# Two steps, one or none of w2's maxima per product, PSUM of h emptied first, and the second filter unit behind a product

## The chip, the cores and the metric

The kernel runs on one core of one Trainium2 chip. What counts is the device time of one execution in microseconds (us), as the median of three runs. A profile of one more execution gives every instruction its place in time; all times below are counted from its first instruction.

## The reference

Two branches read one layer-normed input, and their product is added to the input. One is a filter in two-dimensional frequency space, the other a feed-forward layer with SiLU.

```python
x = A_x                                  # 1 x 2048 x 1024
xn = _layernorm(x, axis=-1)
s = irfft2(rfft2(xn) * (w_r + 1j * w_i)) # the filter, 2048 x 513 complex weights
h = _silu(xn @ B_w1)                     # w1: 1024 x 3584
g = _silu(h @ B_w2)                      # w2: 3584 x 1024
return x + s * g
```

## The kernel before

All matrix work is done in fp16 pairs, a high and a low half of each number, with three matmuls for one product of pairs. TensorE (PE) carries nearly the whole time; VectorE (DVE), ScalarE (ACT) and GpSimd (POOL) do the transforms' butterflies, the splits into halves and the scales; SyncE (SP) issues nearly all DMAs, in order, and waits at each until its data are there.

**Products.** The first layer is 112 products `mm1(c, f)`: a block c of 512 rows times a block f of 128 columns of w1, 24 matmuls into one bank of PSUM (`pa`). From the 25th on, products come in fours: two blocks f for two blocks c, which make one set (q, g) of h. Four PSUM buffers under the tag `ff` take turns, shared with the small matmuls of the column sums (`s`, L290). ACT empties a bank with the SiLU into `h` (L506, `evac`). After the fourth product of a set, `hidden` makes sums and differences of h on DVE (`hr`, L534, L535, L539), and `split` writes the halves of two groups: `hosum` (three arrays) and `hoone` (four). The high half is made on ACT (L281, `high`), the low one on DVE (L284, `low`), and both are stored to `hd` (L528). hosum and hoone have one buffer each.

**Slots.** The order of all engines is written out by the program. Behind each product `after` runs one slot: `settle` (the next stage of each set of h that is under way, then the emptying of the product before), `tick` (deferred DMAs), and `work`: a step of w1's preparation, then a step of the queue `xq`, then up to three steps of the queue `bg`, as long as a sum of estimated DVE costs is not ahead of the sum of PE costs by more than `LEAD`, or until a step returns `PAUSE`. Slots are counted by `count`; product n, counted from 0, has count n - 4.

In `settle` the stages of older sets stand first, and the emptying last:

```python
now, stages[:] = stages[:], []
if fresh_ev[0] is not None:
    now.append(fresh_ev[0])
```

**The queue xq** holds two generators, one after the other. `wmax_gen` takes 25 steps over the filter's weights: a load of 456 KB (`wm`) and a DVE reduction (L997), and a reduction over partitions on POOL. `w2max_gen` takes 31 steps over w2: a load of 128 rows (`w2m`, L403, 512 KB), three steps later the sums or differences of its halves on DVE (`wd`, L407, three buffers), which are stored for later use (`ws`, L408), and a sum of absolute values on ACT (`junk`, L414). Then POOL reduces over partitions. No load of the filter starts before this queue is done.

**The queue bg** holds, in order, the layer norms, the forward transforms `fd_gen(0)` to `fd_gen(3)`, the filter `f_gen` and the inverse transforms. A forward transform ends with four faces (`Rt`, `Ro`), each stored to `rd` (L929, `keep`) and added there once more by an indirect DMA of POOL (L934, `fold`), and for the last two transforms with small stores of an axis (`ao`, L960). Their ends lie near products 47, 67 and 86 for the second, third and fourth.

The filter works in 16 units. It loads data (`vr`, L1032, from `rd`), a table (`kq`, L1025) and weights (`wq`, L1049); `high_v` and `low_v` split vr into the halves of `vq`, on ACT and DVE; `mat` (L1061, `fx`) is the first use on PE. The first products of a unit stand in PE's order behind product 94, so that PE waits there for the low half of vq.

Of the kernel before, what the change touches and what calls it, by code (L numbers as in the profile page):

```python
# [29 lines left out]
SUMMED = (4, 5)  # L30
TURNED = (2, 3)
EXTRA = (20, 21, 22, 24)
ENTRY = ("fbwb||ew", "bbbwwbb|bwbb|f", "fwwbbw|wbbb|wb", "|wew|wf", "w||w")


# [115 lines left out]
def spectral_ffn(ctx, tc, x, w_r, w_i, w1, w2, ca, kc, ci, tw, pm, out):  # L151
# [48 lines left out]
    def defer(n, fn):  # L200
        deferred.append([n, fn])
# [78 lines left out]
    def high(hi, raw, scale):  # L280
        nc.scalar.activation(hi, raw, AF.Copy, scale=scale)  # L281
# [206 lines left out]
    def mm1(c, f, between={}):  # L488
        ps = pf.tile([128, 512], F32, name=f"pa{c}_{f}", tag="ff")
        w, xt = w1t[f], xnT[c]  # L490
        terms = [(d, wh, xh) for wh, xh in ((0, 0), (0, 1), (1, 0)) for d in range(8)]
        if f > 3 or c and f:
            terms.sort(key=lambda k: k[0])
        for n, (d, wh, xh) in enumerate(terms):
            if n in between:
                between[n]()
            nc.tensor.matmul(ps, w[:, wh, d], xt[:, xh, d], start=(n == 0), stop=(n == 23))  # L497
        if c == 3:
            used1.add(f)
        q, g = f // 2, c // 2  # L500

        def evac():
            if (q, g) not in h32:
                h32[q, g] = H["p"].tile([128, 4, 512], F32, name=f"h32_{q}_{g}", tag="h32", bufs=2)
            hq = h32[q, g]
            nc.scalar.activation(hq[:, 2 * (c % 2) + f % 2], ps, AF.Silu, scale=s1[:, f:f + 1])  # L506
            if c % 2 and f % 2:
                return hidden(q, g)

        return evac  # L510

    def hidden(q, g):

        hq = h32.pop((q, g))
        hp = H["p"]
        sc = hs[:, q:q + 1]
        tt = nc.vector.tensor_tensor

        def split(names, src):
            n = len(names)  # L520
            o = hp.tile([128, n, 4, 2, 128], F16, name=f"ho{names[0]}_{q}_{g}", tag=f"ho{n}", bufs=1)
            ov = [o[:, :, :, k] for k in range(2)]
            sv = src.rearrange("f o (p s) -> f o p s", p=4)
            high(ov[0], sv, sc)

            def rest():
                low(ov[1], sv, sc, ov[0])
                defer(2, lambda: nc.sync.dma_start(  # L528
                    hds[SETS.index(names), g][:, :, q].rearrange("f p h s -> f p (h s)"), o.rearrange("f k p h s -> f (k p) (h s)")))

            return rest

        sums = hp.tile([128, 3, 512], F32, name=f"hr{q}_{g}", tag="hr", bufs=1)
        tt(sums[:, 0:2], hq[:, 0::2], hq[:, 1::2], op=OP.subtract)  # L534
        tt(sums[:, 2], hq[:, 0], hq[:, 3], op=OP.subtract)  # L535

        def second():
            rest_s = split(SETS[0], sums)
            tt(hq[:, 2:0:-1], hq[:, 2:4], hq[:, 0:2], op=OP.subtract)  # L539

            def third():
                rest_h = split(SETS[1], hq)
                rest_s()
                return rest_h

            return third

        return second
# [471 lines left out]
    def f_gen():  # L1020
        bp = B["p"]

        def load_k(q):
            t_ = bp.tile([128, 4, 2, 128], F16, name=f"kq{q}", tag="K", bufs=2)
            (nc.sync if q else nc.gpsimd).dma_start(t_, kf[q])  # L1025
            B["k"][q] = t_

        def load_v(u):
            q, j = u // 4, u % 4
            t_ = bp.tile([128, 4, 2, 128], F32, name=f"vr{u}", tag="vr", bufs=2)  # L1030
            for side in range(2):
                nc.sync.dma_start(t_[64 * side:64 * side + 64], rows4[side][j][:, :, q])  # L1032
            raw[u] = t_.rearrange("m c r k -> m c (r k)")
# [3 lines left out]
        def high_v(u):  # L1037
            B["v"][u] = v = bp.tile([128, 4, 2, 256], F16, name=f"vq{u}", tag="vq", bufs=2)
            high(v[:, :, 0], raw[u], 2.0**-22)
# [5 lines left out]
        def load_w(u):  # L1045
            q, j = u // 4, u % 4
            for i in range(2):
                t_ = bp.tile([128, 4, 128], F32, name=f"wq{u}_{i}", tag="wq", bufs=4)
                nc.sync.dma_start(t_, wv[i][q][:, :, 128 * j:128 * j + 128])  # L1049
                B["w"][u, i] = t_  # L1050
# [3 lines left out]
        def mat(u):  # L1054
            q = u // 4
            v, k = B["v"].pop(u), B["k"][q]
            ps = pt.tile([128, 4, 2, 128], F32, name=f"fx{u}", tag="ft")
            for c in range(4):
                o = ps[:, c].rearrange("m r k -> m (r k)")
                for n, (kh, vh) in enumerate(((0, 0), (0, 1), (1, 0))):  # L1060
                    nc.tensor.matmul(o, k[:, c, kh], v[:, c, vh], start=(n == 0), stop=(n == 2))  # L1061
            psx[u] = ps

        load_k(0)
        load_v(0)
        load_w(0)
        yield PAUSE
        load_v(1)
        load_w(1)
        load_k(1)  # L1070
        yield PAUSE
        yield PAUSE
# [14 lines left out]
        def low_z(u):  # L1087
# [3 lines left out]
            if j == 3:  # L1091
                zv = zq.rearrange("m h (c n) i -> m h c (n i)", c=4)
                for c in range(4):
                    defer(1, lambda c=c: nc.sync.dma_start(zd[c][:, q], zv[:, :, c]))

        high_v(0)
        high_v(1)
        yield PAUSE
        low_v(0)
        load_v(2)  # L1100
        yield PAUSE
        mat(0)
        yield 1
        copy(0)
# [423 lines left out]
    def slot(q):  # L1528
        while q:
            job = q[0]  # L1530
            cost = job.step()
            if not job.done:
                return cost
            if q and q[0] is job:
                q.pop(0)
        return 0
# [19 lines left out]
    with tc.manual_schedule():  # L1556
        bg, wq, xq = [], [], []
# [7 lines left out]
        stages, fresh_ev, hold, count = [], [None], [False], [0]  # L1565

        def settle():

            now, stages[:] = stages[:], []
            if fresh_ev[0] is not None:  # L1570
                now.append(fresh_ev[0])
                fresh_ev[0] = None
            for fn in now:
                nx = fn()
                if nx is not None:
                    stages.append(nx)

        def after(ev):
            settle()
            fresh_ev[0] = ev  # L1580
            tick()
            work()

        def work():
            if chunks[0] < 4:
                slot(wq)
            count[0] += 1
            slot(xq)
            clock["dve"] = max(clock["dve"], clock["pe"] - 1.0)
            for _ in range(3):  # L1590
                if clock["dve"] > clock["pe"] + LEAD or hold[0] or slot(bg) == PAUSE:
                    break
            if chunks[0] == 4:
                slot(wq)
# [42 lines left out]
        def do(steps):  # L1637
            for k in steps:
                if k in "fe":
                    todo = early["fe".index(k)]  # L1640
                    todo.pop()(0, ("fe".index(k) and 1 or 3) - len(todo))
                else:
                    slot(wq if k == "w" else bg)
# [7 lines left out]
        for n, (c, f) in enumerate(order):  # L1651
# [3 lines left out]
            if ln[3].done and n >= 21 and not f_job:  # L1655
                add(xq, wmax_gen())
                max_job = add(xq, w2max_gen())
                f_job = add(bg, switch(A, open_f, 1, max_job))
                add(bg, f_gen())
                add(bg, switch(B, open_i, 5, lag=2))  # L1660
                for k in IORDER:
                    add(bg, i_gen(k))
# [14 lines left out]
            while f not in w1t:  # L1677
                slot(wq)
            if n < len(ENTRY):
                enter = [lambda k=k: do(k) for k in ENTRY[n].split("|")]  # L1680
                ev = mm1(c, f, {8: enter[0], 16: enter[1]})
                settle()
                enter[2]()
                fresh_ev[0] = ev
                tick()
                continue
# [4 lines left out]
            after(ev)  # L1691
            if n in EXTRA or left < 4 * LAST and (NFT - 3 not in w1t or left < 20 and not w1j.done) or left < 2 * LAST and (left % 2 or left < 8):
                slot(wq)
        chunks[0], hold[0] = 4, False
        for _ in range(3):
            settle()
            tick()
# [6 lines left out]
        for n, (m, j) in enumerate(seq):  # L1704
# [14 lines left out]
            for k in range(2):  # L1719
                while ready2[0] < m * NP + 7 * k + 6:  # L1720
                    slot(wq)
                mm2(m, j, ps, k)
                if k == 0:
                    settle()
                    load_parts(m, j)
                    ahead_rows(m, j)
                    if (m, j) == (6, 6):
                        load_parts(m, 7)
                        ahead_rows(m, 7)
                    tick()  # L1730
                    work()
# [45 lines left out]
```

## Time and profile before

| | |
|---|---|
| median of three runs | 1228.51 us (1227.4 to 1229.01) |
| the profiled execution's own time | 1228.43 us |
| its span, first to last instruction | 1226.5 us |
| PE busy | 1202.3 us, 98% |
| DVE busy | 1015.4 us, 83% |
| ACT busy | 505.9 us, 41% |
| granted clock of PE, mean | 0.994 |
| DMA, mean over the span | 246 GB/s |

A row of a group or of the timeline names the line, engine, operation and tiles (out<-in), then shapes. The busy share of PE is not the speed of its matmuls: a matmul at a clock of 0.5 is as busy and takes twice as long. Idle time of an engine stands in brackets with the event that ended it; "issue" there means that the profile shows no event.

### The profile page before, as it was taken

The page shows a single profiled execution, that of the slowest core. Times are in us where ns is not written, and L with a number is a line of the kernel's source. Part 1 is how long each engine was busy: PE and PEld are TensorE (multiplying, and loading weights), DVE is VectorE, ACT ScalarE, POOL GpSimd, SP SyncE. Part 2 cuts the span into 40 slices and gives each one's busy share as a digit, 9 for nine tenths or more (in the row PEclk, how much of TensorE's full clock was granted, in tenths as well). Part 3 has the DMA queues.
Part 4 walks back from the last instruction along what each step waited for, and adds up shares of the span by engine and source line. Part 5 has one row for each costly group of instructions (what it writes and reads, how often), then busy time and mean ns, then how long its engine had stood idle before and what let it go on. Part 6 is the DMA issues. An engine that isn't in the chain of part 4 may idle for free.

```text
span 1226.5 us, 18352 instructions
## 1 busy us (share of the span) xinstructions
PE 1202.3 (98%) x6612; PEld 600.1 (49%) x6612; DVE 1015.4 (83%) x1975; ACT 505.9 (41%) x688; POOL 206.3 (17%) x285
## 2 busy tenths in 40 slices
PE   8999999999999979979999999999999999999998
PEld 5544445445444434434444444445455545555555
DVE  7778977986888489648987999999369799898696
ACT  6675554265566444425453332222123222333212
POOL 3320041023002200412110111116132221100000
PEclk9999999999999989999999999999999999999999
DMA  8888797759989994796898999894897998989577
GB/s 252 187 192 206 216 268 198 212 123 277 308 272 297 225 282 132 186 209 168 170 273 225 295 245 267 241 306 152 241 315 221 341 329 314 370 317 330 189 231 269
DMA packets 281331, 302.11 MB, mean 246 GB/s; under 512 B 48244, under 2 KB 207220, under 8 KB 280852
## 3 DMA queue, kind: packets, MB, share of 16 engines
q1 hardware_dynamic: 276808, 289.57, 79.3%
q0 software_dynamic: 4144, 11.23, 4.9%
q8 instruction: 52, 0.85, 0.3%
q14 instruction: 39, 0.32, 0.1%
q10 hardware_dynamic: 288, 0.13, 0.0%
HBM read 183.94 MB, written 110.64 MB: 240 GB/s over the span
## 4 chain that ended last, share of the span: by engine, by line
PE 46%; DMA 9%; DVE 7%; SPq 2%; issue 1%; ACT 1%; POOL 0%; DVEq 0%; POOLq 0%; ACTq 0%
PE pa L497 12%; PE pb L581 10%; PE pb L579 10%; PE pb L580 10%; PE fx L1061 2%; PE id L1427 1%; DMA w<-in_B_w_dram 1%; DMA rd<-Ro 1%; DMA ws<-wd 1%; DMA fs<-sd 1%; DMA rd<-Rt,tws 1%; DMA hd<-hosum 1%; DMA fx<-in_A_x_dram 1%; DMA ht<-hd 1%; DMA sd<-s 1%
## 5 line engine op out<-in xcount | busy, mean ns | idle before, releaser
L497 PE MATMUL pa<-xnT,w 128*128 128x512 f16 x2688 | 588.4, 381 | 4.7 <-ACT h L506 4.0
L497 PEld LDWEIGHTS <-w 128*128 128x128 f16 x2688 | 262.7, 98 | 324.4 <-issue 14.7
L579 PE MATMUL pb<-w,ht 128*128 128x512 f16 (+2 forms) x812 | 300.4, 372 | 0.0
L580 PE MATMUL pb<-w,ht 128*128 128x512 f16 (+2 forms) x812 | 300.4, 372 | 0.0
L581 PE MATMUL pb<-w,ht 128*128 128x512 f16 (+2 forms) x812 | 300.3, 372 | 0.0
L581 PEld LDWEIGHTS <-ht 128*128 128x128 f16 x812 | 79.5, 98 | 91.0
L579 PEld LDWEIGHTS <-ht 128*128 128x128 f16 x812 | 79.6, 98 | 86.5
L580 PEld LDWEIGHTS <-ht 128*128 128x128 f16 x812 | 79.5, 98 | 86.5
L506 ACT ACTIVATE h<-pa,s 128x512 f32<-128x512 f32 x112 | 75.1, 676 | 51.1 <-PE pa L497 40.2
L281 ACT ACTIVATE w<-jr,sc 128x512 f16<-128x512 f32 x98 | 67.8, 713 | 64.5 <-POOL jr L454 44.1
L281 ACT ACTIVATE hosum<-hr,hs 128x1536 f16<-128x1536 f32 x28 | 44.0, 1573 | 99.1 <-DVE hr L535 61.4
L284 DVE SCALAR_TENSOR_TENSOR hoone<-h,hs,hoone 128x2048 f16<-128x2048 f32 x28 | 65.7, 2345 | 15.6 <-ACT hoone L281 15.6
L281 ACT ACTIVATE hoone<-h,hs 128x2048 f16<-128x2048 f32 x28 | 55.9, 1996 | 54.6 <-DMA hd<-hoone 41.6
L284 DVE SCALAR_TENSOR_TENSOR w<-jr,sc,w 128x512 f16<-128x512 f32 x98 | 73.9, 761 | 0.0
L1180 POOL TENSOR_TENSOR Z<-yb 128x32 f32<-128x32 f32 x64 | 34.9, 574 | 219.4 <-DVE yb L1157 219.4
L1085 ACT ACTIVATE zq<-Z,zs 128x1024 f16<-128x1024 f32 x16 | 18.4, 1148 | 95.4 <-DVE Z L1180 58.7
L454 POOL TENSOR_TENSOR jr<-jr,w 128x512 f32<-128x512 f32 x28 | 38.7, 1385 | 107.6 <-DMA w<-in_B_w_dram 60.2
L284 DVE SCALAR_TENSOR_TENSOR hosum<-hr,hs,hosum 128x1536 f16<-128x1536 f32 x28 | 50.8, 1814 | 4.6 <-ACT hosum L281 4.6
L673 ACT ACTIVATE pl<-pl,c 128x512 f32<-128x512 f32 (+2 forms) x28 | 17.4, 654 | 73.6 <-DVE pl L649 42.4
L284 DVE SCALAR_TENSOR_TENSOR w<-w1r,rs,w 128x1024 f16<-128x1024 f32 x28 | 35.7, 1276 | 12.1 <-ACT w L281 12.1
L534 DVE TENSOR_TENSOR hr<-h 128x1024 f32<-128x1024 f32 x28 | 34.2, 1222 | 11.7 <-ACT h L506 11.7
L281 ACT ACTIVATE w<-w1r,rs 128x1024 f16<-128x1024 f32 x28 | 31.9, 1141 | 25.5 <-DVE w L284 19.7
(239 smaller groups left out, 1537.6 us busy)
## 6 DMA issues: line engine op xcount, KB each, us to landing
ht<-hd SPq DMA_DIRECT2D x112, 448.0 KB
hd<-hoone SPq DMA_DIRECT2D x28, 1024.0 KB
hd<-hosum SPq DMA_DIRECT2D x28, 768.0 KB
w1r<-in_B_w_dram SPq DMA_DIRECT2D x28, 512.0 KB
w2m<-in_B_w_dram SPq DMA_DIRECT2D x28, 512.0 KB
jr<-in_B_w_dram SPq DMA_DIRECT2D x56, 256.0 KB
ws<-wd SPq DMA_DIRECT2D x42, 256.0 KB
jr<-ws SPq DMA_DIRECT2D x42, 256.0 KB
```

The lines of the kernel that those rows point to most:

```text
L281: nc.scalar.activation(hi, raw, AF.Copy, scale=scale)
L284: nc.vector.scalar_tensor_tensor(lo, raw, scale, hi, op0=OP.mult, op1=OP.subtract)
L454: nc.gpsimd.tensor_tensor(raw[n], raw[n], more.pop(n), op=OP.add)
L497: nc.tensor.matmul(ps, w[:, wh, d], xt[:, xh, d], start=(n == 0), stop=(n == 23))
L506: nc.scalar.activation(hq[:, 2 * (c % 2) + f % 2], ps, AF.Silu, scale=s1[:, f:f + 1])
L534: tt(sums[:, 0:2], hq[:, 0::2], hq[:, 1::2], op=OP.subtract)
L579: nc.tensor.matmul(ps, hh[:, 0], w[:, 0], start=first, stop=False)
L580: nc.tensor.matmul(ps, hh[:, 0], w[:, 1], start=False, stop=False)
L581: nc.tensor.matmul(ps, hh[:, 1], w[:, 0], start=False, stop=last)
L1061: nc.tensor.matmul(o, k[:, c, kh], v[:, c, vh], start=(n == 0), stop=(n == 2))
L1085: nc.scalar.activation(zqs[q][:, 0, :, 16 * j:16 * j + 16], zs_[u], AF.Copy, scale=zs)
L1180: eng.tensor_tensor(Z[:, ns, pos], x0[:, :, ls], x1[:, :, ls], op=o_)
```

## The change

Three things. First, a table: in the slots with counts 28 to 33 the queue xq takes two steps, in each third slot from 48 to 78 none, else one as before. So wmax_gen ends six products earlier, w2max_gen starts at product 40 and not at 46, runs one step per product to 51 and two in three from 52 on, and ends at 81 and not at 77. Second, `evac` is given back as two functions: the emptying of PSUM, which `settle` now runs ahead of the older stages, and the rest (the start of `hidden`), which keeps its place. Third, in `f_gen` the load of the first unit's weights moves behind the loads of vr and kq, and the second unit's split and load of weights move behind the next product.

```diff
+TWICE, THIRD = range(28, 34), range(48, 80, 3)
...
             nc.scalar.activation(hq[:, 2 * (c % 2) + f % 2], ps, AF.Silu, scale=s1[:, f:f + 1])
+
+        def rest():
             if c % 2 and f % 2:
                 return hidden(q, g)
 
-        return evac
+        return evac, rest
...
         load_k(0)
         load_v(0)
-        load_w(0)
         yield PAUSE
         load_v(1)
-        load_w(1)
         load_k(1)
...
+        load_w(0)
         high_v(0)
-        high_v(1)
         yield PAUSE
         low_v(0)
         load_v(2)
         yield PAUSE
+        high_v(1)
+        load_w(1)
         mat(0)
...
             if fresh_ev[0] is not None:
-                now.append(fresh_ev[0])
+                if type(fresh_ev[0]) is tuple:
+                    first, rest = fresh_ev[0]
+                    first()
+                    now.append(rest)
+                else:
+                    now.append(fresh_ev[0])
                 fresh_ev[0] = None
...
             count[0] += 1
-            slot(xq)
+            for _ in range(2 if count[0] in TWICE else 0 if count[0] in THIRD else 1):
+                slot(xq)
```

What the order of the instructions becomes is shown at three places. ACT around products 72 to 75, before; `hosum_8_1` and `hoone_8_1` are the halves of the set made by products 68 to 71, `h_9_0` is the set of products 72 to 75, `L_3_2` belongs to the fourth transform:

```order
L281 ACTIVATE hosum_8_1_4259<-hr_1_4219,hs 128x12x128
L506 ACTIVATE h_9_0_4262<-pa_18_4193,s_222 128x512
L414 ACTIVATE junk,w2m<-w2m_4092 128x1024
L281 ACTIVATE hoone_8_1_4298<-h_8_1_4038,hs 128x16x128
L506 ACTIVATE h_9_0_4262<-pa_19_4234,s_222 128x512
L414 ACTIVATE junk,w2m<-w2m_4172 128x1024
L844 ACTIVATE L_3_2_4332<-fa_2_4097 128x8x65
```

And after, from the same h on:

```order
L507 ACTIVATE h_9_0_4252<-pa_18_4185,s_222 128x512
L282 ACTIVATE hosum_8_1_4254<-hr_1_4211,hs 128x12x128
L847 ACTIVATE L_3_2_4285<-fa_2_4092 128x8x65
L848 ACTIVATE L_3_2_4285<-fa_2_4092 128x8x63
L507 ACTIVATE h_9_0_4252<-pa_19_4227,s_222 128x512
L282 ACTIVATE hoone_8_1_4328<-h_8_1_4035,hs 128x16x128
L415 ACTIVATE junk,w2m<-w2m_4049 128x1024
```

Each h stands ahead of hosum or hoone now, and one of the two steps over w2 is gone from the stretch.

SP in the third transform's end and behind it, before, from a store of hoone on (`ws_8` to `ws_10` are stores of w2's sums, `rd<-ao` the axis, `hd_0` the stores of the hidden layer):

```order
L408 DMA ws_10_144<-wd_23_4051 128x512
L408 DMA ws_10_172<-wd_23_4053 128x512
L403 DMA w2m_4092<-in_B_w_dram 128x1024
L528 DMA hd_0_90<-hosum_8_0_4035 1536x1x256
L408 DMA ws_10_158<-wd_24_4094 128x512
L303 DMA w1r_4168<-in_B_w_dram 128x8x128
L303 DMA w1r_4170<-in_B_w_dram 128x8x128
L403 DMA w2m_4172<-in_B_w_dram 128x1024
L960 DMA rd_3_78<-ao_3891 8x128
L960 DMA rd_3_82<-ao_3891 8x128
L528 DMA hd_0_92<-hoone_8_0_4081 2048x1x256
```

And after:

```order
L409 DMA ws_10_144<-wd_23_4051 128x512
L409 DMA ws_10_172<-wd_23_4053 128x512
L531 DMA hd_0_90<-hosum_8_0_4037 1536x1x256
L304 DMA w1r_4162<-in_B_w_dram 128x8x128
L304 DMA w1r_4164<-in_B_w_dram 128x8x128
L404 DMA w2m_4166<-in_B_w_dram 128x1024
L963 DMA rd_3_78<-ao_3900 8x128
L963 DMA rd_3_82<-ao_3900 8x128
L531 DMA hd_0_92<-hoone_8_0_4082 2048x1x256
```

A load of w2 went from ahead of the store of hosum, and a store of ws from between the two stores of the hidden layer.

ACT at the filter's start, before (`vq_5113` and `vq_5115` are the first and second unit's high halves, `w_26` and `w_27` w1's):

```order
L281 ACTIVATE vq_5113<-vr_4969 128x4x256
L281 ACTIVATE vq_5115<-vr_5007 128x4x256
L281 ACTIVATE w_26_5117<-w1r_4914,rs_221 128x1024
L281 ACTIVATE hosum_11_0_5144<-hr_0_5099,hs 128x12x128
L506 ACTIVATE h_12_0_5147<-pa_24_5073,s_222 128x512
L281 ACTIVATE w_27_5150<-w1r_4916,rs_221 128x1024
L281 ACTIVATE hoone_11_0_5182<-h_11_0_5004,hs 128x16x128
L506 ACTIVATE h_12_0_5147<-pa_25_5119,s_222 128x512
L1079 ACTIVATE xc_5199<-fx_5186 128x512
```

And after:

```order
L282 ACTIVATE vq_5109<-vr_4969 128x4x256
L282 ACTIVATE w_26_5111<-w1r_4914,rs_221 128x1024
L507 ACTIVATE h_12_0_5138<-pa_24_5065,s_222 128x512
L282 ACTIVATE hosum_11_0_5140<-hr_0_5091,hs 128x12x128
L282 ACTIVATE w_27_5144<-w1r_4916,rs_221 128x1024
L507 ACTIVATE h_12_0_5138<-pa_25_5113,s_222 128x512
L282 ACTIVATE hoone_11_0_5177<-h_11_0_4997,hs 128x16x128
L282 ACTIVATE vq_5180<-vr_5003 128x4x256
L1080 ACTIVATE xc_5199<-fx_5186 128x512
```

The second vq stands seven rows later, ahead of the copy `xc` of the first unit's products. DVE keeps its order there: the low half of `w_26`, then that of the first vq. On SP the two loads of the first unit's wq stand behind the loads of vr and kq and behind two stores of the hidden layer, and those of the second unit behind the third load of vr.

## The prediction

> **What bounds the kernel now.** I read the page's head first, then who TensorE waits for, then stretches around those waits. The head:
>
> ```profile
> span 1226.5 us, 18352 instructions
> PE 1202.3 (98%) x6612; PEld 600.1 (49%) x6612; DVE 1015.4 (83%) x1975; ACT 505.9 (41%) x688; POOL 206.3 (17%) x285
> ```
>
> TensorE (PE) is the bound: 24.2 us of the span are not matmuls. A change can win those, and the matmul time lost to a lower clock; no more. The waits of PE up to 560 us (who waited for whom: total, times, longest), then PE's busy time and granted clock in stretches around them (length, busy, count, clock, DMA share, GB/s):
>
> ```profile
> PE fx L1061 <- DVE vq L284: 5.2, 1, 5.2
> PE s L290 <- ACT h L506: 4.2, 2, 3.2
> PE pa L497 <- ACT h L506: 4.0, 3, 2.4
> ...
> 434.00:438.00 4.00, 2.84 (x14) 1.00 0.98 289
> 441.00:448.00 7.00, 1.40 (x7) 0.92 1.01 340
> 448.00:454.00 6.00, 6.00 (x16) 0.52 0.60 191
> 533.00:537.00 4.00, 2.57 (x13) 1.00 0.34 85
> 546.00:552.00 6.00, 0.83 (x5) 0.77 1.12 316
> 552.00:557.00 5.00, 5.00 (x21) 0.59 0.74 198
> ```
>
> Three holes. At 434 to 454: 1.16 + 5.60 us idle, then 6 us at clock 0.52, which loses 6 x 0.48 = 2.9: **9.6 us**. At 533: **1.4 us**, no loss of clock. At 546: 5.2 us idle, then 5 x 0.41 = 2.0 and 0.2 ahead of 552: **7.4 us**. Together 18.5 us. In the first two PE waits for ScalarE (ACT) to empty a bank of PSUM (h L506), in the third for the low half of the first filter unit (vq).
>
> Why ACT was late at the first hole, and in the last row at the second (timeline of ACT; in brackets the idle time and what ended it):
>
> ```profile
> 434.52 1.58 ACT L281 ACTIVATE hosum<-hr,hs 128x1536 f16<-128x1536 f32 x1 [10.27 <-DMA hd<-hosum]
> 436.01 0.67 ACT L506 ACTIVATE h<-pa,s 128x512 f32<-128x512 f32 x1
> 442.61 2.00 ACT L281 ACTIVATE hoone<-h,hs 128x2048 f16<-128x2048 f32 x1 [4.90 <-DMA hd<-hoone]
> 444.52 0.67 ACT L506 ACTIVATE h<-pa,s 128x512 f32<-128x512 f32 x1
> 447.09 0.69 ACT L506 ACTIVATE h<-pa,s 128x512 f32<-128x512 f32 x1
> ...
> 532.64 2.00 ACT L281 ACTIVATE hoone<-h,hs 128x2048 f16<-128x2048 f32 x1 [18.30 <-DMA hd<-hoone]
> ```
>
> hosum and hoone have one buffer each, so each waits until the store of the last one has landed, and the h of the same slot stands behind it. Those stores were late because VectorE (DVE) was late, and DVE because of w2's maxima (SPq is SyncE's queue, here in the act of issuing):
>
> ```profile
> 398.49 11.68 SPq L408 DMA_DIRECT2D ws<-wd  x2
> 401.03 0.69 DVE L407 TENSOR_TENSOR wd<-w2m 128x512 f32<-128x512 f32 x1 [4.38 <-DMA ws<-wd]
> 413.91 0.69 DVE L407 TENSOR_TENSOR wd<-w2m,w2m 128x512 f32<-128x512 f32 x1 [11.05 <-issue]
> 417.43 0.69 DVE L407 TENSOR_TENSOR wd<-w2m 128x512 f32<-128x512 f32 x1 [2.83 <-DMA ws<-wd]
> ...
> 435.87 0.57 SPq L528 DMA_DIRECT2D hd<-hoone  x1
> ```
>
> With three wd buffers a step of the maxima waits for the ws store of three before; SP sat 11.7 us over two of these stores, and DVE stood 18.3 us in three waits.
>
> **The change, part by part.** No instruction is added or removed; bytes and busy times stay.
>
> *The table.* A step of w2max_gen is one load of w2, on average 1.5 stores of ws, 1.5 subtractions or additions of 0.69 us on DVE and 1.05 us on ACT; a step of w's maxima is a load of 128 x 912 numbers (456 KB) and a reduction:
>
> ```profile
> w2m<-in_B_w_dram SPq DMA_DIRECT2D x28, 512.0 KB
> ws<-wd SPq DMA_DIRECT2D x42, 256.0 KB
> L414 ACT ACTIVATE junk<-w2m 128x1024 fp8e4<-128x1024 f32 x28 | 29.4, 1049 | 3.2 <-DMA w2m<-in_B_w_dram 3.0
> L997 DVE TENSOR_REDUCE mw<-wm 128x1 f32<-128x912 f32 x18 | 19.8, 1097 | 0.0
> ```
>
> A step of w2's maxima so moves 896 KB. Before, products 46 to 77 carry one each; after, 40 to 51 carry one each and 52 to 81 two in three. The price in the place that gets them is read from stretches of all engines (busy of PE, PEld, DVE, ACT, POOL; clock; DMA share; GB/s):
>
> ```profile
> 240.00:280.00 40.00, 40.00 (x188) 18.14 (x187) 35.82 (x76) 22.60 (x28) 9.10 (x7) 1.00 0.60 152
> 280.00:320.00 40.00, 40.00 (x259) 21.09 (x258) 27.47 (x67) 21.26 (x31) 8.27 (x10) 1.00 1.02 297
> 320.00:360.00 40.00, 40.00 (x188) 18.11 (x186) 38.04 (x95) 26.45 (x39) 0.82 (x2) 1.00 0.95 299
> 400.00:440.00 40.00, 38.84 (x217) 18.97 (x216) 22.06 (x43) 16.48 (x22) 7.18 (x9) 1.00 0.93 244
> ```
>
> At 297 GB/s a step costs 3.0 us of the DMA. Six steps move ahead of 284 us, 18 us, where 0.40 x 40 = 16 us were free, and the loads of w's maxima leave that stretch. It fits, just. The six second steps of w's maxima at products 32 to 37 (1.1 us of DVE each) are in the planner's sum, which puts steps of the second transform two products later; the third and fourth transforms end at products 67 and 86 as before. So I cost them at nothing: what hides them is PE's row of products, 40.00 of 40 us busy from 240 to 400; uncovered they would be 6.6 us of lateness on DVE. POOL's two reductions, one six products earlier and one four later, have users far behind. What is won: between 330 and 440 us every third step goes, 58 GB/s out of 244 to 299. In the jam itself, from the store of hoone 7_1 to that of 8_1 on SP, there stood 12 ws and 6 w2m, now 7 and 6: 1.3 MB or some 4 us less, and less is queued when it begins. My estimate for the two is that the late stores land 6 to 9 us earlier, bounds 0 (the jam is the transform's own) and 18 (DVE's three waits go altogether); I take the middle because the share there was 0.93, near full.
>
> *PSUM first.* With the h ahead in its slot, the bank awaited by the product at 436.7 is empty before the 10.27 us wait, and the one behind it at 436.8 instead of 444.5. What remains with unchanged stores is the next product's bank, empty at about 445.3; PE, not held at 436, would come at 441.0 and wait 4.3 us in place of 6.8. So this part alone wins 2.5 us of idle time, and the two parts together need the stores only 4.3 us earlier: the whole 9.6 us goes. The 1.4 us at 533 are the same order, an h behind the hoone that waited 18.30 us; one h more is ahead of it now, and a product takes longer than 1.4 us, so they go. Added waits: hosum and hoone now stand behind an h that may wait for its product; ACT is 41% busy and is the late one in these stretches, so I take nothing. The bounds: no gain, since nothing moves ahead but the h; one h of 0.67 us for each hosum or hoone, which delays DVE's low half and the store, not PE.
>
> *Filter unit 1 behind a product, w(0) and w(1) later.* ACT, DVE and PE at the third hole:
>
> ```profile
> 540.92 1.06 ACT L281 ACTIVATE vq<-vr 128x1024 f16<-128x1024 f32 x1 [4.55 <-DMA wq<-in_A_w_r_dram]
> 547.05 1.06 ACT L281 ACTIVATE vq<-vr 128x1024 f16<-128x1024 f32 x1 [5.07 <-DMA vr<-rd]
> 548.01 1.13 ACT L281 ACTIVATE w<-w1r,rs 128x1024 f16<-128x1024 f32 x1
> 549.18 1.28 DVE L284 SCALAR_TENSOR_TENSOR w<-w1r,rs,w 128x1024 f16<-128x1024 f32 x1 [8.47 <-ACT w L281]
> 550.38 1.22 DVE L284 SCALAR_TENSOR_TENSOR vq<-vr,vq 128x1024 f16<-128x1024 f32 x1
> 551.65 1.65 PE L1061 MATMUL fx<-vq,kq 128*128 128x256 f16 x7 [5.17 <-DVE vq L284]
> ```
>
> ACT's second vq waited for its load; w1's split stood behind it, DVE in order behind that, then the low half PE wants. Taken out: 541.98 + 1.13 + 1.28 + 1.22 = 545.6. Two loads of w(0), 0.5 MB, no longer go between: at 297 GB/s 1.8 us, so 543.8. But PE now comes earlier: 546.2 less 9.6 and 1.4 is 535.2. The low half must come 8.6 us earlier still, and it hangs on the transform's end:
>
> ```profile
> 501.82 0.42 DVE L271 TENSOR_TENSOR Ro<-Rb 128x256 f32<-128x256 f32 x1
> 507.35 1.26 SPq L929 DMA_DIRECT2D rd<-Ro  x1
> 520.89 1.51 POOL L934 DMA_INDIRECT rd<-Ro,tws  x1 [6.63 <-DMA rd<-Ro]
> 534.38 1.19 SPq L1032 DMA_DIRECT2D vr<-rd  x2
> ```
>
> From the last butterfly to the load are 32 us of transfers, which I leave as they are. That butterfly moves with DVE, which loses fewer of its 18.3 us: by 6 to 10 us. The wait left is between 0 (543.8 - 10 is ahead of 535.2) and 4.4 us (545.6 - 6 - 535.2); I take **2 us**, short of the 5.2 us after which the clock fell. The loads of w(0) now stand behind two hd stores on SP; eight instructions of the unit come ahead of their user on DVE, so I take nothing, and at most the 6.5 us that the load of vr took (534.38 to 540.92), on DVE.
>
> Sum: 1228.4 (the profiled execution's own time, 0.1 under the median of 1228.5) - 9.6 - 1.4 - 7.4 + 2.0 = **1212 us**. Behind 560 us PE and DVE both start some 16 us earlier, so the rest shifts.
>
> **The skill's clock rule.** The holes of 1.2 and 1.4 us kept clock 1.00; those of 5.6 and 5.2 us were followed by about 6 us near 0.5. The Trainium skill, TensorE: Matmul & The Clock Gate, Part 1: The HAM clock gate, says the array falls to half rate after an idle window of about 3.4 us and comes back after as long a busy one. The trace agrees with it at 1.4 and 5.2 us; between them no row here decides. By that rule a remainder of 2 us costs 2 us, and one of 4.3 us, as PSUM first alone would leave, keeps the whole loss of 2.9; a gate that still held at 4.3 us would make that second case 1215.7 instead of 1218.6.
>
> **Rivals.**
> - The transform's end does not come earlier (its 32 us of transfers stretch): PE stands from 535.2 to 543.8, 8.6 us, and loses 2.2 of clock, so 10.8 for 7.4: 1228.4 - 9.6 - 1.4 + 3.4 = 1220.8. For it: the DMA share near 1 there; against: fewer bytes.
> - The table does nothing for the jam; PSUM first and the filter part act alone: 2.5 + 1.4 (4.3 us of standing keeps the loss of clock, being nearer 5.2 than 1.4), PE at the filter unit at 542.3, wait 1.5, 5.9 won: 1218.6. For it: SP's order in the jam lost only stores. Against: the share of 0.95 ahead of it falls.
> - Slower: the jam moves to the end of the second transform, 280 to 320 us, where the share is 1.02 already and six steps more come before. If wd's waits cost DVE there the 18 us they cost at 400, it can't catch up at 38.04 of 40 us busy, so that the old holes stay and a new one of 9.6 us is added: 1238. It decides if DVE's idle time there grows from 12.5 to over 25 us. Against: 12.5 us idle cost PE nothing.
> - Nothing moves, because other waits fill the slots: 1228.
>
> **How the numbers follow.** 0.60 for the sum's case (own range 1209 to 1216), 0.13 for 1220.8, 0.10 for 1218.6, 0.09 for no change, 0.08 for slower. 1209 is all holes gone with half a us of scatter in favour; up to 1222 the two middle cases are in, so 0.83 lies inside. A measurement tells 0.2% (2.5 us) from no change: faster 0.83, same 0.09, slower 0.08.
>
> **What would show it.** Right: no PE wait for h between 400 and 460 us and clock 1.00 there; DVE's waits of wd between 395 and 420 us under 10 us in all; fx's wait for vq under 3 us; DMA share of 240 to 280 us up to 0.9 and of 320 to 400 down to 0.8. Wrong: PE waits between 260 and 340 us, or fx waiting 8 us for vq, or wd's waits unchanged and a hole of 4 us followed by half clock.

## The result and the profile after

The changed kernel takes **1214.95 us** (median of six runs, 1211.77 to 1218.84), the one before 1229.79 (six runs, 1227.40 to 1232.04): a ratio of 0.988, interval 0.9854 to 0.9906, so some 15 us less. The forecast was 1212.0 with a range of 1209 to 1222 and 0.83 for faster. The profiled execution of the changed kernel is the longest of its six, 1218.84 us; a second one of the same kernel is among the experiments.

Head, and the longest of TensorE's waits up to 560 us (who waited for whom: total, times, longest):

```profile
span 1217.0 us, 18354 instructions
PE 1199.7 (99%) x6612; PEld 599.3 (49%) x6612; DVE 1014.8 (83%) x1975; ACT 505.9 (42%) x688; POOL 205.4 (17%) x285
...
PE pa L498 <- ACT h L507: 3.1, 1, 3.1
```

The wait for vq and the waits of the jam at 434 to 454 us are gone. One wait for h is left, and it is longer than what stood there before: 3.1 us at 524, for 1.4 at 533. The first two rows are the stretches behind that wait and behind a new one at 882 us (length, busy, count, clock, DMA share, GB/s); the others are the stretches whose loads the table moved (there busy and count of PE, PEld, DVE, ACT and POOL first):

```profile
527.50:534.00 6.50, 6.50 (x23) 0.74 1.08 248
886.00:892.00 6.00, 6.00 (x39) 0.72 0.99 377
...
240.00:280.00 40.00, 40.00 (x188) 18.16 (x187) 38.01 (x87) 24.84 (x34) 4.50 (x4) 1.00 0.85 255
...
320.00:360.00 40.00, 40.00 (x202) 18.66 (x200) 39.38 (x106) 25.59 (x34) 0.94 (x3) 1.00 0.90 274
...
400.00:440.00 40.00, 40.00 (x223) 19.60 (x221) 24.72 (x60) 17.83 (x26) 6.89 (x10) 1.00 0.91 250
```

The six steps fit: 0.60 became 0.85 at 240 to 280 us, and TensorE stands nowhere from 240 to 440. The jam itself is as full as before (0.91 for 0.93). What changed in it is who is late. DVE's waits between 385 and 440 us, before and then after:

```profile
DVE wd L407 <- issue: 11.0, 1, 11.0
DVE wd L407 <- DMA ws<-wd: 8.1, 3, 4.4
```

```profile
DVE bf L868 <- DMA rd<-Rt,tws: 14.5, 1, 14.5
DVE hr L537 <- ACT h L507: 4.4, 1, 4.4
```

DVE stands as long as before (21 us in sum), but now mostly once, at the start of the fourth transform's butterflies, and no longer in wd step after step. The low half of hoone, and with it the store that the next hoone waits for, is still behind that long wait, but less work lies between the two (8.9 us before, 3.3 after). DVE before, then DVE and SP after:

```profile
426.31 2.35 DVE L284 SCALAR_TENSOR_TENSOR hoone<-h,hs,hoone 128x2048 f16<-128x2048 f32 x1
```

```profile
419.76 2.34 DVE L285 SCALAR_TENSOR_TENSOR hoone<-h,hs,hoone 128x2048 f16<-128x2048 f32 x1
...
427.29 0.57 SPq L531 DMA_DIRECT2D hd<-hoone  x1
```

The low half comes 6.5 us earlier, and the store (at 435.87 us before) 8.6 us earlier. ACT's hosum and hoone, after:

```profile
426.56 1.57 ACT L282 ACTIVATE hosum<-hr,hs 128x1536 f16<-128x1536 f32 x1 [3.65 <-DVE hr L538]
434.68 2.00 ACT L282 ACTIVATE hoone<-h,hs 128x2048 f16<-128x2048 f32 x1 [5.00 <-DMA hd<-hoone]
```

Each starts 8 us earlier (434.52 and 442.61 before), ahead of the moment when TensorE wants the bank behind it.

The new wait far behind, at 882 us, is for the first inverse transform's input. DVE's copy into zt ends the wait for the load, TensorE's iu follows it:

```profile
885.42 0.21 DVE L1310 COPY zt<-zps 128x16 f16<-128x16 f16 x1 [15.87 <-DMA w<-in_B_w_dram]
...
885.73 1.96 PE L1341 MATMUL iu<-kk,zt 128*128 128x128 f16 x24 [3.97 <-DVE zt L1310]
```

(The bracket names a load on the same queue that landed then. That the copy waits for the load of zt is read from the program: the copy reads zps and writes into the tile that this load fills.) Before, that copy stood 10.87 us and came just in time. The loads of zt were issued 13.6 us earlier than before (863.3 for 876.9 us), but the copy came only 9.2 earlier (885.42 for 894.64).

**One table for all that follows.** All products are alike, so the start of the n-th of the 112 products in the timeline, less that of the same product before, says how far TensorE is ahead or behind, clock included. The columns are differences of that lead: over the jam (products 66 to 86), over the hole at 533 us (86 to 94), over the filter unit (94 to 96), and from the last product to the end of the span. Negative is time won. One profiled execution each. Left out are 0 to 1.0 us of difference ahead of product 66, and what changes between product 96 and the last one: nothing, except -1.3 in twice_only and +0.4 in third_only.

| kernel | median us | ratio to before, interval | jam | at 533 | filter | behind |
|---|---|---|---|---|---|---|
| changed kernel | 1214.95 | 0.988 (0.9854 to 0.9906) | -10.1 | +3.2 | -7.5 | +4.7 |
| again: the same | 1214.83 | 0.9866 (0.9836 to 0.9897) | -7.0 | +3.0 | -7.5 | +0.4 |
| psum_only | 1231.04 | 1.0004 (0.9987 to 1.0021) | +4.2 | +0.7 | -1.4 | +5.4 |
| table_only | 1221.03 | 0.9917 (0.9887 to 0.9947) | -8.8 | +2.5 | -6.1 | +5.3 |
| filter_only | 1225.91 | 0.9966 (0.9947 to 0.9986) | +1.6 | +4.0 | -7.5 | +1.7 |
| no_psum | 1213.61 | 0.9878 (0.9853 to 0.9903) | -10.1 | -0.7 | -7.5 | +2.6 |
| no_table | 1226.50 | 0.9977 (0.9961 to 0.9993) | +1.1 | -1.5 | -7.5 | -0.7 |
| no_filter | 1217.96 | 0.9914 (0.9891 to 0.9937) | -9.4 | -0.2 | -1.5 | -0.7 |
| store_early | 1216.20 | 0.9892 (0.9864 to 0.9920) | -9.5 | +5.4 | -7.5 | +1.1 |
| iu_later | 1217.86 | 0.9913 (0.9889 to 0.9936) | -10.1 | -0.5 | -7.5 | +3.8 |
| twice_only | 1234.18 | 1.0032 (1.0014 to 1.0050) | +1.4 | +10.7 | -7.5 | +0.9 |
| third_only | 1240.49 | 1.0079 (1.0056 to 1.0101) | -8.1 | +11.9 | -2.5 | +13.2 |
| skip_jam | 1217.65 | 0.9902 (0.9876 to 0.9928) | -7.3 | -1.2 | -7.5 | +0.8 |

The changed kernel, again and iu_later have the same order up to the last product: their rows say how much one execution differs from the next (3 us in the jam, 3.7 at 533). A profiled execution need not be a typical one: that of psum_only is the longest of its thirteen (1237.38 us), that of no_table the shortest of its twelve (1220.04).

### The profile page after: what moved, and what is told of

It reads as the page before. It is cut to its first block, busy times and chain, and to the rows that moved or that the text cites. A ratio compares the mean times of both kernels' runs of the same rounds, so it can differ in the third digit from the quotient of the medians.

```text
span 1217.0 us, 18354 instructions
## 1 busy us (share of the span) xinstructions
PE 1199.7 (99%) x6612; PEld 599.3 (49%) x6612; DVE 1014.8 (83%) x1975; ACT 505.9 (42%) x688; POOL 205.4 (17%) x285
## 4 chain that ended last, share of the span: by engine, by line
PE 64%; DVE 17%; DMA 14%; issue 2%; SPq 1%; ACT 1%; POOL 1%; POOLq 0%; DVEq 0%; ACTq 0%
PE pa L498 27%; PE pb L582 10%; PE pb L583 10%; PE pb L584 10%; DMA rd<-Rt,tws 3%; DMA rd<-V 2%; DMA w<-in_B_w_dram 2%; PE fx L1064 2%; DMA jr<-in_B_w_dram 2%; DVE w L285 1%; DVE hoone L285 1%; PE id L1430 1%; DVE wd L408 1%; DMA w2m<-in_B_w_dram 1%; DMA fs<-sd 1%
## 5 line engine op out<-in xcount | busy, mean ns | idle before, releaser
L1183 DVE TENSOR_TENSOR Z<-yb 128x128 f32<-128x128 f32 (+1 forms) x128 | 42.3, 399 | 0.0
```

The costliest lines, as they stand in the source:

```text
L1183: eng.tensor_tensor(Z[:, ns, pos], x0[:, :, ls], x1[:, :, ls], op=o_)
```

## The experiments

**The same kernel once more (again).** No edit.

> The changed kernel itself, nothing edited, for its scatter and a second profiled execution. Theory A: its runs scatter (1211.8 to 1218.8 us) because the load of zt ahead of the first inverse transform lands with 0 to 5 us of jitter, so an execution below 1214 us shows no wait of TensorE for zt near 882 us (4.0 us in the first profiled execution of 1218.84 us), while the wait of 3.1 us for h at 524 us stays in all. Theory B: the 524 us wait is what scatters; then a run below 1214 us shows no wait there and the zt wait stays. Median 1213 to 1217 us either way.

Median 1214.83, six runs from 1210.95 to 1218.18; the profiled one took 1218.18, so the question about a fast one stayed open. Its waits:

```profile
PE pa L498 <- ACT h L507: 3.9, 2, 2.9
...
PE pa L498 <- DVE e L317: 1.8, 1, 1.8
PE iu L1341 <- issue: 1.2, 1, 1.2
```

As long as the first execution, but with the time in other places: the wait for zt only 1.2 us, and 3 us lost in the jam instead. So neither theory: by these two executions the scatter of 7 us lies in several waits, not in one.

**Each part alone.** Before, with one part of the diff above each: psum_only the two functions of `evac` and their call, table_only the table and the loop over it, filter_only the lines of `f_gen`.

```diff
# psum_only
+                    first, rest = fresh_ev[0]
+                    first()
+                    now.append(rest)
# table_only
-            slot(xq)
+            for _ in range(2 if count[0] in TWICE else 0 if count[0] in THIRD else 1):
+                slot(xq)
# filter_only
+        load_w(0)
         high_v(0)
-        high_v(1)
...
+        high_v(1)
+        load_w(1)
         mat(0)
```

> Before with the part PSUM first alone. The prediction's working: the first hole falls from 9.6 to 7.2 us (a wait of 4.3 us, and half clock behind it stays), the 1.4 us at 533 us go, the third hole of 7.4 us stays or grows by up to 3.8 us because TensorE comes to the filter unit earlier: 1228.4 - 2.4 - 1.4 = 1224.6 us, up to 1228.4. Rival: the h moved ahead is all that is needed at both places: first hole gone too, 1217.4 us if the third hole doesn't grow.

> Before with the table alone. Theory A: in the changed kernel hoone near 440 us starts 7.9 us earlier than before, and DVE's waits of wd are gone; if the table does that, the first hole goes also with h behind hoone in its slot (-9.6 us). TensorE then comes 9.9 us earlier to the product at 533 us while its hoone comes some 7.8 us earlier, so that the 1.4 us there become 3.5 us and half clock behind them costs 2 more; the third hole falls from 7.4 to 2 us or so: 1228.4 - 9.6 + 4.1 - 5.4 = 1217.5 us. Rival (the jam is the transform's own, the table does nothing there): 1226 to 1228 us with the first hole as before.

> Before with the filter part alone. Theory A: the third hole goes whole (5.2 us of waiting and 2.2 of clock), since the low half comes at 543.8 us and TensorE, not helped by the other parts, only at 546.2 us: 1221.0 us, both other holes as before (9.6 and 1.4). Rival: the low half hangs on the load of vr and not on the order: a wait of 2 to 4 us stays, 1223 to 1227 us.

PSUM first alone: 1.0004, nothing (between 1.6 us less and 2.6 more). TensorE, DVE and ACT in the jam of its profiled execution:

```profile
446.53 0.18 PE L290 MATMUL s<-m1b,unit 128*128 128x2 bf16 x1 [5.59 <-DVE m1b L309]
452.86 7.41 PE L497 MATMUL pa<-xnT,w 128*128 128x512 f16 x23 [6.14 <-ACT h L506]
...
445.25 1.22 DVE L309 TENSOR_REDUCE m1b<-w1r 128x1 bf16<-128x1024 f32 x1
...
448.22 2.00 ACT L281 ACTIVATE hoone<-h,hs 128x2048 f16<-128x2048 f32 x1 [4.93 <-DMA hd<-hoone]
450.13 1.04 ACT L414 ACTIVATE junk<-w2m 128x1024 fp8e4<-128x1024 f32 x1
...
452.12 0.68 ACT L506 ACTIVATE h<-pa,s 128x512 f32<-128x512 f32 x1
```

The first, short wait goes. Then TensorE wants w1's column sum s, whose maximum DVE makes only by 446.5 us, and then the bank of the next product, whose h ends at 452.8. That last one decides: the wait for s costs nothing, since TensorE would have stood until 452.8 without it. This h stands behind the same hoone as before, with a step over w2 and two copies L between them. With the stores late, one h ahead of hoone does not help: the prediction's 2.4 and 1.4 us fall, and so does the rival's whole hole. Why hoone itself started 5.6 us later here than before (448.22 for 442.61) stays open.

The table alone: 1221.03, and the jam's hole goes with h still behind hoone. Theory A's time is 3.5 us off (the wait for zt took 5.2 us in its profiled execution, which A had at nothing). The filter part alone: 1225.91, 4.4 us under before's 1230.3 of the same comparison, for the 7.4 expected. Its own column is -7.5, with no wait for vq, so not the rival; in its profiled execution 1.6 and 4.0 us more were lost in the two holes ahead and 1.7 behind.

**One part undone.** The changed kernel without one of its parts, the same lines taken back.

```diff
# no_psum
-                    first, rest = fresh_ev[0]
-                    first()
-                    now.append(rest)
+                now.append(fresh_ev[0])
# no_table
-            for _ in range(2 if count[0] in TWICE else 0 if count[0] in THIRD else 1):
-                slot(xq)
+            slot(xq)
# no_filter
-        load_w(0)
         high_v(0)
+        high_v(1)
...
-        high_v(1)
-        load_w(1)
         mat(0)
```

> The changed kernel with the part PSUM first undone (table and filter part stay). Theory A (alone it moved the median by 0.0%, and the table alone took the first hole with h behind hoone): worth nothing or little here too, 1214 to 1217 us, the hole at 524 us some 0 to 2 us longer. Theory B (the prediction's: it takes the waits that are shorter than a product): with h behind hoone the waits near 440 and 524 us come back by 1.4 to 3.5 us each, and half clock behind them: 1218 to 1222 us.

> The changed kernel with the table undone (PSUM first and the filter part stay). The prediction's rival case gave 1218.6 us for these two parts. Theory A (the late stores of the jam are the cause and the two parts only move the wait): as the filter part alone, 1224 to 1227 us, with 9 to 15 us lost between 434 and 456 us. Theory B (order on ACT is the cause): 1218 to 1220 us.

> The changed kernel with the filter part undone (table and PSUM first stay). Theory A: the wait for the low half comes back but small, since DVE and the transform's end come 10 us earlier and TensorE 6 to 7: 0 to 2 us, no half clock; with the table alone it was 1.3 us. 1215 to 1218 us. Theory B (the filter part is worth by itself here what it is worth alone, 0.34% or 4.2 us): 1219 us.

Without PSUM first 0.9878, the same as with it (0.988 and 0.9866): theory A, though the hole at 524 us was not longer but smaller (-0.7 in its column). Without the table 0.9977, within theory A's 1224 to 1227: the other two parts are worth 0.2%, not the 1218.6 us that the prediction's second rival gave them. Without the filter part 0.9914 (1218.0 us), so the part is worth some 0.4% here as it is alone. That is theory A's time, at its end, but not its mechanism: TensorE, 9.4 us ahead when it comes there, waits 4 us and not 0 to 2, with the half clock behind it (0.72 from 541 to 547 us):

```profile
PE fx L1064 <- DVE vq L285: 4.1, 1, 4.1
```

**The hole at 524 us (store_early).**

```diff
-                defer(2, lambda: nc.sync.dma_start(
+                defer(1 if (q, g, n) == (10, 0, 4) else 2, lambda: nc.sync.dma_start(
```

> The changed kernel with one store moved: that of hoone 10_0 stands on SP ahead of the two loads of w1 and the four stores of ao instead of behind them (at 515.0 us in the first profiled execution of the changed kernel, though its data was ready at 497.1). Theory A: the store lands by 512 us, hoone 10_1 no longer waits 15.3 us, the hole of 2.9 to 3.1 us at 524 us goes with some 1.7 us of clock; TensorE then reaches the filter unit 3 to 5 us earlier, where 3.4 us of slack stood: 3 to 4.7 us faster than the changed kernel, 1210 to 1212 us. Rival (the transfers are full there, and the store lands late wherever it stands): the hole stays, or moves to hosum or to the filter unit's vq, 1214 to 1216 us.

In the changed kernel SP and ACT looked so there:

```profile
498.37 6.20 SPq L304 DMA_DIRECT2D w1r<-in_B_w_dram  x2
506.56 8.37 SPq L963 DMA_DIRECT2D rd<-ao  x4
515.02 0.91 SPq L531 DMA_DIRECT2D hd<-hoone  x1
...
524.83 2.00 ACT L282 ACTIVATE hoone<-h,hs 128x2048 f16<-128x2048 f32 x1 [15.31 <-DMA hd<-hoone]
```

And with the store ahead of the loads of w1:

```profile
500.38 2.54 SPq L531 DMA_DIRECT2D hd<-hoone  x1
502.97 18.54 SPq L304 DMA_DIRECT2D w1r<-in_B_w_dram  x2
...
524.77 1.22 DVE L310 TENSOR_REDUCE m1b<-w1r 128x1 bf16<-128x1024 f32 x1 [21.60 <-DMA w1r<-in_B_w_dram]
...
528.31 0.18 PE L291 MATMUL s<-m1b,unit 128*128 128x2 bf16 x1 [3.02 <-DVE m1b L310]
```

The store went at 500 us, and now SP stood 18.5 us over w1's loads: DVE, with the hidden layer's halves behind it, waited for w1, and TensorE for the column sum. 0.9892 (1216.2 us) is no gain over the changed kernel, and the hole is longer (5.4 for 3.0 to 3.2 in the table). The rival holds: with the store early, w1's loads are late in its place.

**The scatter behind the products (iu_later).**

```diff
-                add(bg, switch(B, open_i, 5, lag=2))
+                add(bg, switch(B, open_i, 6, lag=2))
```

> The changed kernel with one number more: the first inverse transform's matmuls stand one slot of the second product's sequence (about 5 us of TensorE) further behind the load of zt. Theory A: that load lands with a jitter of 0 to 5 us in every kernel (TensorE waited for it 0 us in the one execution of before, 4.0 and 1.2 in two of the changed kernel, 3.0 with PSUM first alone, 5.2 with the table alone), and this is a part of the scatter; a slot later no execution waits there: median 1211 to 1213.5 us, no wait of iu, runs within 5 us. Theory B: what comes behind hangs on that transform's chain, and a slot later ends a slot later: 1216 to 1220 us.

1217.86 us: 3 us over the changed kernel's 1214.95 and 1214.83, with intervals that overlap (0.9889 to 0.9936 beside 0.9854 to 0.9906 and 0.9836 to 0.9897). The wait of iu is gone, and theory A falls all the same; the time is theory B's, whose chain no trace here shows. The longest of TensorE's waits behind 700 us, in the profiled execution, the shortest of the six:

```profile
PE pb L582 <- DMA ht<-hd: 2.1, 1, 2.1
```

In this execution the time of the one wait stands in others: 2.1 us here, with half clock behind it, and 1.2 us at id.

**The table's halves.** twice_only, then third_only:

```diff
-TWICE, THIRD = range(28, 34), range(48, 80, 3)
+TWICE, THIRD = range(28, 34), ()
...
-TWICE, THIRD = range(28, 34), range(48, 80, 3)
+TWICE, THIRD = (), range(48, 80, 3)
```

> The changed kernel with half of the table: the six second steps of w's maxima stay, no step of w2's maxima is left out; these then stand one to a product from 40 to 70 and are through at some 405 us, ahead of the jam. Theory A (what counts is how many bytes of w2's maxima lie between 400 and 450 us): the first hole is as small as in the changed kernel or smaller; 1212 to 1216 us. Theory B (what counts is that 320 to 400 us are thinned, so that the third transform ends early enough): the share there is as high as before, 0.95 or more, the jam is queued up when it begins, and 4 to 9 us stay lost at the first hole: 1219 to 1224 us.

> The changed kernel with the other half of the table: no second steps of w's maxima, but every third step of w2's left out from product 52 on; these stand from 46 to 87, and the filter stage opens one product later. Theory A (the thinning is what counts): the first hole goes as with the whole table, the opening one product later costs 0 to 5 us at the filter unit: 1214 to 1219 us. Theory B (the six steps ahead are what counts): 1220 to 1226 us.

Both have longer times than before: 1.0032 and 1.0079. Neither theory had that. With the six steps ahead alone, w2's maxima are through at 405 us and the first hole is as large as before (+1.4), as theory B had it, so it is not only the bytes between 405 and 450 us that count; and in the fourth transform's end w1's last two loads fall behind the axis' stores on SP:

```profile
521.77 7.76 SPq L963 DMA_DIRECT2D rd<-ao  x4
529.62 1.31 SPq L304 DMA_DIRECT2D w1r<-in_B_w_dram  x2
...
534.05 1.22 DVE L310 TENSOR_REDUCE m1b<-w1r 128x1 bf16<-128x1024 f32 x1 [20.87 <-DMA w1r<-in_B_w_dram]
...
545.03 7.10 PE L498 MATMUL pa<-xnT,w 128*128 128x512 f16 x24 [7.26 <-ACT h L507]
```

With the thinning alone the first hole goes (-8.1: it is the thinning that takes it), but the steps now run to product 87, into the end of the fourth transform, where SP stands over stores of ws again:

```profile
504.73 4.97 SPq L409 DMA_DIRECT2D ws<-wd  x2
...
537.78 17.73 PE L498 MATMUL pa<-xnT,w 128*128 128x512 f16 x72 [7.73 <-ACT h L507]
```

**Where to thin (skip_jam).**

```diff
-TWICE, THIRD = range(28, 34), range(48, 80, 3)
+TWICE, THIRD = range(28, 34), range(62, 72)
```

> The changed kernel with the empty places of the table put elsewhere: in place of every third product from 52 to 79, the ten products 66 to 75 (some 378 to 435 us) carry no step of w2's maxima; before and after them one to a product; the six second steps stay, and the last step stands at product 80 as before this edit. So the same number of steps lies ahead of 284 us and none in the jam. Theory A (bytes of w2's maxima in the jam are what counts): the first hole goes as in the changed kernel, DVE has no wait of wd between 385 and 435 us; 1212 to 1216 us. Theory B (what counts is DVE's and the DMA's load between 300 and 380 us, where the third transform is made; thinning the jam alone comes too late, as one to a product up to 405 us did): half or more of the first hole stays, and the fourth transform ends no earlier: 1219 to 1226 us.

1217.65, 0.9902: theory A for the jam, with another price. DVE has no wait of wd there and the jam's own hole is gone, but at one step a product 320 to 400 us is fuller than in the changed kernel (DMA share 0.95 and 0.90 for 0.90 and 0.87):

```profile
320.00:360.00 40.00, 40.00 (x205) 18.86 (x204) 37.56 (x98) 24.04 (x36) 0.93 (x3) 1.00 0.95 298
360.00:400.00 40.00, 38.28 (x179) 17.30 (x178) 36.14 (x68) 24.34 (x37) 3.98 (x2) 1.00 0.90 278
```

TensorE stands 1.7 us between 360 and 400, where it stood nowhere in the changed kernel. Beside twice_only this tells where the jam is decided: up to product 65 the two have the same steps, twice_only five more at products 66 to 70 (378 to 405 us), skip_jam the same five at 76 to 80; skip_jam wins 7.3 us in the jam, twice_only none. So the jam hangs on how many steps stand at 378 to 405 us.

## Why the prediction was right, point by point

**The first hole, -9.6.** Right in sum: -10.1, -7.0 and -10.1 in three executions of this order. The table carries it alone (table_only, no_psum). The store's lead was taken as 6 to 9 us; hoone started 7.9 us earlier (434.68 for 442.61). The way there is another than the one forecast: DVE does not lose "fewer of its 18.3 us", it stands 21 us between 385 and 440 us in both kernels, and the long wait ends at the same time (416.5 us for 417.4). What moved is the work behind it. The share came out at 0.85 ("up to 0.9") in 240 to 280 us, and at 0.90 in 320 to 360, not down to 0.8: by these rows what was won lies in the order of SP and DVE, not in a lighter jam.

**PSUM first, -2.5 alone.** Wrong: alone and undone it moves nothing that the intervals can tell. The step that failed is "the next product's bank, empty at about 445.3". That puts its h right behind hoone (442.61 + 2.0 + 0.67), but a step over w2 and two copies L stand between, as the order of ACT shows: in psum_only h ends 4.6 us after hoone starts, which by the times before is 447.2 us. The product started at 447.83 before, so this part could win some 0.6 us (an estimate from these rows), and both parts together need the stores some 6 us earlier and not 4.3; they came 7.9 earlier. The added waits were not nothing either: an h ahead of hoone waits until DVE has read the older h out of one of the two buffers, 18.6 us in four waits in the changed kernel and none before; TensorE had no wait behind those in the jam.

**The 1.4 us at 533.** Wrong: +3.2, +3.0 and -0.5 in three executions; even in the third a wait of 1.1 us is left. Two steps failed. TensorE's lead of 9.9 us was set against the filter unit, but not here: hoone came only 7.8 us earlier (524.83 for 532.64), which makes 1.4 + 2.1 = 3.5 us. And "one h more is ahead, a product takes longer than 1.4 us" holds only if a product lies between two claims on PSUM. Here before and after (TensorE's timeline):

```profile
535.27 0.16 PE L290 MATMUL s<-m1b,unit 128*128 128x2 bf16 x1 [1.02 <-ACT h L506]
535.85 4.48 PE L497 MATMUL pa<-xnT,w 128*128 128x512 f16 x20 [0.41 <-ACT h L506]
```

```profile
524.17 0.17 PE L291 MATMUL s<-m1b,unit 128*128 128x2 bf16 x1
527.45 2.87 PE L498 MATMUL pa<-xnT,w 128*128 128x512 f16 x8 [3.12 <-ACT h L507]
```

The column sum takes a bank of the same four, and the bank won went to it; the product wants the next one 0.2 us later, behind the hoone. How long that is scatters with the store: without PSUM first (no_psum) hoone started at 521.87 us, and 0.7 us of waiting were left.

**The filter unit, -7.4 + 2.0.** The part does what was said, and the remainder that I took at 2 us is 0: -7.5 in nine of the ten profiled executions that have it, in the tenth (third_only) the filter opens a product later. The last butterfly moved by 10.3 us (491.51 for 501.82, and its store on SP, rd<-Ro, 497.03 for 507.35), the top of the 6 to 10, and the order without the second vq in it did the rest: with the old order (no_filter) 4.1 us of waiting stay. The low half ends at 536.06 us and fx starts at 539.50. (The wait before began at 551.65 - 5.17 = 546.5 us, not at 546.2; the 0.3 us change nothing.)

```profile
531.50 1.06 ACT L282 ACTIVATE vq<-vr 128x1024 f16<-128x1024 f32 x1 [3.52 <-DMA vr<-rd]
...
534.84 1.22 DVE L285 SCALAR_TENSOR_TENSOR vq<-vr,vq 128x1024 f16<-128x1024 f32 x1
...
539.50 1.47 PE L1064 MATMUL fx<-vq,kq 128*128 128x256 f16 x12
```

**"Behind 560 us the rest shifts."** Not in the profiled execution, which gave 4.7 us back there, 4.0 of them waiting for zt. That this is a price of the change is not shown: the same wait was 3.0 us with PSUM first alone, where TensorE is later than before, and 5.2, 1.2 and 0 elsewhere; before's one profiled execution had none.

In sum, for the profiled execution: -10.1 + 0.2 (its start) + 3.2 - 7.5 + 4.7 = -9.5, the difference of the spans (1217.0 for 1226.5). By the medians it is -14.8 and -15.5, for -16.4 forecast. The misses, the 1.4 us that became 3 and the 2 us that became 0, partly cancel: that the sum came out so near is in part luck.

**The rivals.** The first, that the transform's end comes no earlier, fell with the butterfly's 10.3 us. The second, that the table does nothing, fell with table_only and no_table. The slower one, the jam moving to 280 to 320 us, didn't come: no wait of TensorE there. A new jam is possible at another place: cut either half off the table, and one at 520 to 545 us costs 11 to 12 us. Open stay what in the planner's sums puts w1's loads there, and the 13.2 us that third_only lost behind the products, 7.5 of which are waits for the loads of ht.

## What to carry to other kernels

Time won at one hole is owed at the next: set TensorE's lead against every later chain that comes near it, and count every claim on the pool (here a column sum's bank, 0.2 us ahead of the product's) and every instruction that stands between (here a step over w2 and two copies), before a better order is called enough. In this kernel moving one store changed who is late, not how long; what helped was to take whole steps out of the stretch just ahead of the jam and to put as many where the DMA had room, so that none spilled into the next jam. And one profiled execution places waits no better than its scatter, here 3 to 5 us a place: read a small term from several.

## What the runs showed of the hardware

The half clock comes in steps of one length. In each execution that shows it ahead of the last matmuls, it lasts 3.41 us or a whole multiple of that, and its starts and ends lie whole multiples apart: before, they are at 446.89, 453.72, 549.29 and 556.12 us, that is 2, 30 and 32 times 3.413 us behind the first. So time can be cut into windows of 3.41 us, and what counts is how long TensorE is busy in one window, not how long one wait is. Rows of again, iu_later and psum_only, cut at these windows (length, busy, count, clock, DMA share, GB/s):

```profile
528.81:532.23 3.42, 1.07 (x5) 1.00 0.60 157
532.23:535.64 3.41, 3.41 (x9) 0.50 1.15 234
```

```profile
877.51:880.92 3.41, 1.34 (x7) 1.00 1.03 394
880.92:884.33 3.41, 3.41 (x9) 0.50 1.03 398
```

```profile
897.83:901.24 3.41, 1.82 (x9) 1.00 1.08 265
901.24:904.66 3.42, 1.96 (x27) 1.00 1.03 396
```

In iu_later a wait of 2.07 us lies in one window and is followed by half clock. In psum_only a wait of 2.95 us is parted by the end of a window at 901.24, and the clock stays at 1.00, behind it too. In all profiled executions that show a half clock, and behind their first 12 us, a window at full clock with up to 1.34 us busy was followed by one at half clock (21 times), and one with 1.49 us or more never. So the prediction's reading, waits of 1.4 us keep the clock and waits of 5.2 us lose it, leaves out where in the window the wait falls. The Trainium skill, TensorE: Matmul & The Clock Gate, Part 1: The HAM clock gate, puts the half clock behind an idle window of about 3.4 us that runs freely. The trace agrees with the length, and with windows that do not start at the wait; but the window need not be idle, since 1.34 us of work in it did not keep the clock, and there the measurement decides.

A window at half clock costs 1.7 us where TensorE has work throughout, as behind the 3.1 us in the changed kernel and the 4.0 us at 882. Before, the hole of 5.6 us had two such windows, and TensorE still stood for 0.9 us of them, so 2.9 us were lost.
